# One h @ w_in per later batch on four column groups, spread by transfers, and more groups ahead of the exponentials and the first scores

## The chip, the cores and the metric

The kernel runs on one core of a Trainium2 chip. The metric is the device time of one execution in microseconds (us), as the median of several executions. Five engines run their own queues in order: TensorE (PE in the rows, with its weight loads as PEld), VectorE (DVE), ScalarE (ACT), GpSimd (POOL) and the queue that issues the transfers (SP). They meet at semaphores only.

## The reference, cut to what matters

```python
def mab(q, kv):                                   # attention_out = mab(x, mab(inducing, x))
    s = q @ kv.transpose(0, 2, 1) / np.sqrt(C)
    s = s - s.max(-1, keepdims=True)
    a = np.exp(s)
    a /= a.sum(-1, keepdims=True) + 1e-09
    return a @ kv
h = mab(I, x)                # per batch: 32 inducing points read all 12480 tokens: h is 32 x 128
x = mab(x, h)                # per token: 32 scores, softmax, then a mix of the 32 rows of h
h1 = x @ w_in                # the tokens of 4 batches, 49920 x 128, through 128 x 2048
g = h1 * (1.0 / (1.0 + np.exp(-1.702 * h1)))
out = g @ w_out              # 2048 x 128
```

All is float32, with 4 batches of 12480 tokens. The kernel never forms the attention output: it multiplies `h @ w_in` once per batch (32 x 2048), and the weights of a token's softmax then pick from that product.

## The kernel before, in words

**The main loop.** The tokens lie in blocks of 512, and each block takes eight **groups**, one for every 256 of the 2048 hidden columns; there are 98 blocks, and so 784 groups, numbered `i` from 0 to 783. `first(i)` makes two matmuls `ph<-st,hw` (the softmax weights `st` of the block against `hw`, which is h @ w_in) into one of two `ph` buffers of PSUM, and lets ScalarE write the activation `g`. Its rounded copy `hi` is made by ScalarE from `ph` once more, or by VectorE from `g`; a running account of both engines' costs decides which when the program is built. VectorE then makes the remainder `lo` from `g` and `hi`. `second(i, c)` makes three matmuls into `pso` for each half of a group, six for a group. A `ph` buffer comes free when ScalarE has read it the last time, so the first layer of group i+2 waits for ScalarE's `g` or `hi` of group i.

**The lag.** The second layer of a group follows its first layer by a lag of 6 to 12 half groups. Attention work that takes ScalarE some time hands back the word `LUMP` (line 24): the loop then runs all second-layer work down to a lag of 6 at once, 18 matmuls beyond the usual six, and lets the lag grow again by one half group in every third group. Such a third group has three second-layer matmuls instead of six; I call it a short group. So after each lump 18 groups follow of which six are short.

**Attention in the gaps.** `attention(b)` for batches 1 to 3 is a generator. The loop takes one step of it per group (`next(rest, None)`, line 806), and `hop(n)` inside it stands for n groups of waiting. For one batch it makes, in this order: loads of `xt`; first scores `pa<-xt,indT_sb` of seven pieces of the batch in pairs, copied out by VectorE as `s` with their maximum `mx`; exponentials of four pieces and later three, each with a lump; the weighted sum `pa<-xn,aT`; the small matrix `hT`; second scores `pa<-xt,hT` in pairs, which VectorE transposes into `e` and reduces; their exponentials on ScalarE, of four pieces and then of three, each with a lump. Between gelu and exp ScalarE loads another table each way. `pairs` works through the pieces in the order 0 to 6 for even batches and 6, 0 to 5 for odd ones.

**The lay-out.** `weights_of(b, s)` turns the exponentials of one piece into `st` for four blocks: VectorE sums and divides (`sm`, `e<-e,sm`), transposes to `alT`, ScalarE or VectorE rounds that to `ahT`, VectorE takes the remainder, and 16 transfers spread both. It begins at fixed groups that the loop works out in `begin` (lines 780 to 800): 18, 50, 82, 114, 146, 162, 174, 186, 218 and so on. Where the exponentials that it needs are not yet there, `lay_out` runs the attention generator on until they are (`while key not in es: next(rest)`), and drops what the generator hands back.

**h @ w_in.** `h_w_in(b, c)` makes one of four products of 512 columns. For batches 1 to 3 the table `products` puts them at four groups shortly before and after the batch's first block (186, 188, 190 and 193 for batch 1). `hTs[b]` holds the 32 columns of h four times over, so that each product comes out on all 128 partitions; ScalarE rounds it into `hw`, and VectorE replaces the lower half by the remainder.

Of the kernel before, what the change touches and what calls it, by code (L numbers as in the profile page):

```python
# [8 lines left out]
F32 = mybir.dt.float32  # L9
# [46 lines left out]
def set_attention_then_moe(ctx: ExitStack, tc, xT, x, indT, w_in, w_out, outT):  # L56
# [36 lines left out]
    pe = ctx.enter_context(tc.tile_pool(name="pe", bufs=EB))  # L93
    pt = ctx.enter_context(tc.tile_pool(name="pt", bufs=7))
    pst = ctx.enter_context(tc.tile_pool(name="pst", bufs=G))
    phw = ctx.enter_context(tc.tile_pool(name="phw", bufs=7))
    psm = ctx.enter_context(tc.tile_pool(name="psm", bufs=3))
    ps_h = ctx.enter_context(tc.tile_pool(name="ps_h", bufs=2, space=PSUM))
    ps_o = ctx.enter_context(tc.tile_pool(name="ps_o", bufs=2, space=PSUM))
# [98 lines left out]
    def attention(b):  # L198
# [3 lines left out]
        if not start:  # L202
            for s in range(XB):
                load_xT(b, s)
                yield

        mx = psm.tile([P, NS], F32, tag="mx", name="mx")
        rs = psm.tile([P, NS], F32, tag="rs", name="rs")
# [36 lines left out]
        def maximum(n):  # L245

            mx1 = psm.tile([P, 1], F32, tag="mx1", name="mx1")
            dve.tensor_reduce(mx1, mx[:, 0:n], axis=AX.X, op=ALU.max)
            yield from wait()
            pa = ps_a.tile([P, 512], F32, tag="pa", name="pa")  # L250
            pe_.matmul(pa[0:1, 0:P], mx1, ident, start=True, stop=True)
            yield
            row = psm.tile([1, G, M], F32, tag="row", name="row")
            dve.tensor_reduce(
                row[:, 0, :], pa[0:1, 0:P].rearrange("p (g m) -> p m g", g=G), axis=AX.X, op=ALU.max
            )
            for j in range(1, G):
                dve.tensor_copy(row[:, j, :], row[:, 0, :])
            yield from wait()
            pa = ps_a.tile([P, 512], F32, tag="pa", name="pa")  # L260
            pe_.matmul(pa[:, 0:1], row.rearrange("p g m -> p (g m)"), one, start=True, stop=True)
            yield
            nmx = psm.tile([P, 1], F32, tag="nmx", name="nmx")
            dve.tensor_scalar(nmx, pa[:, 0:1], -scale, None, op0=ALU.mult)
            yield from wait(2)
            return nmx
# [234 lines left out]
            ready.append(True)  # L501
        yield
        for some in (turn[2:],) if start else (turn[0:4], turn[4:]):
            yield from hop(20 if start else 8)
            for pair in pairs(some):
                while full(pair):
                    yield
# [2 lines left out]
                for s, pa in zip(pair, pas):  # L510
                    if s + XB < NS:
                        again(s + XB)
                    mine[s] = yield from second_out(s, pa)
                yield from wait(2)
            for s in some:
                exponentials(s, mine[s])
            yield LUMP

    def h_w_in(b, c):

        if b == 0:
            if c % 2 == 0:
                first_h.append(ps_h.tile([P, 2, 512], F32, tag="ph", name="ph"))
            pa = first_h[-1][:, c % 2]
        else:
            pa = ps_a.tile([P, 512], F32, tag="pa", name="pa")
        pe_.matmul(pa, hTs[b], w_in_sb[:, c * 512:(c + 1) * 512], start=True, stop=True)
        yield
        t = phw.tile([P, 512], F32R, tag="hw", name="hw")
        act.copy(t, pa)  # L530
        dve.tensor_sub(t[P // 2:P], pa[P // 2:P], t[P // 2:P].bitcast(F32))
        hw[b, c] = t

    def weights_of(b, s):

# [217 lines left out]
            yield from attention(b)  # L753

    n = len(work) * NG

    products = []
    for b in range(1, B):
        f = first_block[b, NS - 1 if b % 2 else 0] * NG
        products += [(f + at, b, c) for c, at in enumerate((-6, -4, -2, 1) if b % 2 else (-7, -5, -3, -1))]  # L760
    rest = attentions()
    act.t = dve.t = pe_.t
    back = part = laid = None
    stores = []
    under_way = []
    turns.pop(0)
# [14 lines left out]
    while i < n or under_way:  # L781
        now[0] = i
        if i < n:
# [5 lines left out]
                if turns and first_block[turns[0]] * NG <= i:  # L789
                    back, laid = lay_out()  # L790
            first(i)
            if part is not None:
                run(part)
                part = None
            if products and products[0][0] == i:
                part = h_w_in(*products.pop(0)[1:])
                next(part)
            under_way += [(i, 0), (i, 1)]
            i += 1
        else:  # L800
# [46 lines left out]
```

## Time and profile before

| | |
|---|---|
| median of 3 executions | 1628.84 us (1627.38 to 1629.14) |
| the profiled execution | 1631.19 us, of which its span is 1629.4 us |
| TensorE, VectorE, ScalarE busy | 98%, 83%, 83% of the span |
| chain of work that ended last | TensorE 90%, VectorE 3%, ScalarE 3% |
| first group of the main loop | starts at about 72 us |

A busy share of TensorE in these rows counts matmuls whose modelled ends overlap the next start, so it does not tell whether matmuls follow each other as closely as they can. That is read from the distance between starts, and above all from the distance between the first-layer matmuls `ph<-st,hw` of one group and the next. Counting those from the first one on gives every group its place in time: group 179, for example, starts at 430.73 us.

### The profile page before, as it was taken

The page shows a single profiled execution, that of the slowest core. Times are in us where ns is not written, and L with a number is a line of the kernel's source. Part 1 is how long each engine was busy: PE and PEld are TensorE (multiplying, and loading weights), DVE is VectorE, ACT ScalarE, POOL GpSimd, SP SyncE. Part 2 cuts the span into 40 slices and gives each one's busy share as a digit, 9 for nine tenths or more (in the row PEclk, how much of TensorE's full clock was granted, in tenths as well). Part 3 has the DMA queues.
Part 4 walks back from the last instruction along what each step waited for, and adds up shares of the span by engine and source line. Part 5 has one row for each costly group of instructions (what it writes and reads, how often), then busy time and mean ns, then how long its engine had stood idle before and what let it go on. Part 6 is the DMA issues. An engine that isn't in the chain of part 4 may idle for free.

```text
span 1629.4 us, 21749 instructions
## 1 busy us (share of the span) xinstructions
PE 1593.6 (98%) x7737; PEld 1236.1 (76%) x7737; DVE 1346.0 (83%) x1556; ACT 1352.4 (83%) x1552; POOL 32.0 (2%) x26
## 2 busy tenths in 40 slices
PE   6799999999999999999999999999999999999999
PEld 3577777787777877777777877778778888888887
DVE  6787977888889887788888887878888888888886
ACT  6498888978888888887888888988889988888885
POOL 4300000000000000000000000000000000000000
PEclk9799999999999999999999999999999999999999
DMA  8304218503042114741204101661301011011010
GB/s 338 104 24 159 72 30 187 136 26 98 18 142 84 35 39 86 180 100 39 72 26 190 39 30 46 158 152 40 97 16 48 20 38 46 22 38 45 28 38 20
DMA packets 81946, 126.65 MB, mean 78 GB/s; under 512 B 11632, under 2 KB 50096, under 8 KB 75696
## 3 DMA queue, kind: packets, MB, share of 16 engines
q1 hardware_dynamic: 81840, 125.26, 27.0%
q8 instruction: 63, 1.03, 0.3%
q14 instruction: 43, 0.35, 0.1%
HBM read 74.10 MB, written 25.56 MB: 61 GB/s over the span
## 4 chain that ended last, share of the span: by engine, by line
PE 90%; DVE 3%; ACT 3%; issue 1%; DMA 1%; POOL 1%; SPq 0%; DVEq 0%; ACTq 0%; POOLq 0%
PE pso L46 63%; PE ph L46 22%; PE pa L46 4%; ACT hi L46 1%; DMA xt<-in_xT 1%; ACT g L46 1%; DVE lo L46 1%; DVE e L46 1%; DVE t L46 0%; DVE m L46 0%; ACT s L46 0%; DMA out_T<-ob 0%; DVE alT L46 0%; POOL sq L592 0%; POOL wh L642 0%
## 5 line engine op out<-in xcount | busy, mean ns | idle before, releaser
L46 DVE TENSOR_TENSOR lo<-g,hi 128x1024 fp32r<-128x1024 f32 (+1 forms) x784 | 947.8, 1216 | 156.7 <-ACT hi L46 143.9
L46 ACT ACTIVATE g<-ph 128x1024 f32<-128x1024 f32 (+1 forms) x784 | 805.7, 1033 | 200.3 <-PE ph L46 104.5
L46 PE MATMUL pso<-hi,wl 128*128 128x512 f32 (+1 forms) x1568 | 623.7, 398 | 0.0
L46 PE MATMUL pso<-hi,wh 128*128 128x512 f32 (+1 forms) x1568 | 617.3, 394 | 0.0
L46 PE MATMUL pso<-lo,wh 128*128 128x512 f32 (+1 forms) x1568 | 616.8, 393 | 0.0
L46 PE MATMUL ph<-st,hw 128*128 128x512 f32 x1536 | 491.8, 401 | 8.6 <-ACT hi L46 4.5
L46 ACT ACTIVATE hi<-ph 128x1024 fp32r<-128x1024 f32 (+1 forms) x476 | 488.7, 1027 | 0.0
L46 PEld LDWEIGHTS ph<-st,hw 128*128 128x128 f32 x1536 | 282.0, 188 | 103.1 <-ACT hi L46 16.8
L46 PEld LDWEIGHTS pso<-lo,wh 128*128 128x128 f32 x1568 | 294.4, 188 | 73.3 <-issue 2.9
L46 PEld LDWEIGHTS pso<-hi,wl 128*128 128x128 f32 x1568 | 295.2, 188 | 70.4 <-issue 2.9
L46 PEld LDWEIGHTS pso<-hi,wh 128*128 128x128 f32 x1568 | 294.9, 188 | 70.7
L46 DVE CAST hi<-g 128x1024 fp32r<-128x1024 f32 (+1 forms) x308 | 210.5, 684 | 92.5 <-ACT g L46 92.0
L46 ACT COPY ob<-pso 128x512 f32<-128x512 f32 (+1 forms) x98 | 58.1, 593 | 19.8 <-PE pso L46 19.7
L46 PE MATMUL pa<-xt,indT_sb 128*32 128x512 f32 x192 | 25.8, 641 | 13.5 <-DMA xt<-in_xT 11.1
L46 ACT ACT_TABLE_LOAD x28 | 35.9, 1283 | 2.1 <-PE ph L46 0.9
L46 ACT CAST ahT<-alT 128x512 fp32r<-128x512 f32 (+1 forms) x27 | 15.7, 582 | 14.7 <-DVE alT L46 14.6
L46 PE MATMUL pa<-xt,hT 128*32 128x512 f32 x192 | 25.5, 637 | 1.0 <-DVE hT L46 1.0
L46 PEld LDWEIGHTS pa<-xt,indT_sb 128*32 128x32 f32 x192 | 4.8, 111 | 24.6 <-issue 14.4
L46 ACT ACTIVATE e<-e 128x512 f32<-128x512 f32 (+1 forms) x28 | 14.2, 571 | 9.0 <-DVE e L46 8.9
L46 PEld LDWEIGHTS pa<-xn,aT 128*32 128x32 f32 (+1 forms) x594 | 15.1, 109 | 7.6 <-issue 5.8
L46 PE MATMUL pa<-xn,aT 128*32 128x128 f32 (+1 forms) x594 | 20.7, 276 | 0.0
L46 ACT ACTIVATE s<-s,nmx 128x512 f32<-128x512 f32 (+1 forms) x28 | 18.5, 662 | 2.4 <-DVE nmx L46 2.3
(93 smaller groups left out, 434.3 us busy)
## 6 DMA issues: line engine op xcount, KB each, us to landing
xt<-in_xT SPq DMA_DIRECT2D x48, 1024.0 KB, 7.7
out_T<-ob SPq DMA_DIRECT2D x96, 256.0 KB, 2.0
xn<-in_x SPq DMA_DIRECT2D x72, 256.0 KB, 6.1
st<-ahT SPq DMA_DIRECT2D x192, 64.0 KB, 2.0
st<-alT SPq DMA_DIRECT2D x192, 64.0 KB, 2.0
raw<-in_w_in SPq DMA_DIRECT2D x4, 512.0 KB, 8.9
raw<-in_w_out SPq DMA_DIRECT2D x4, 512.0 KB, 8.1
xt_last<-in_xT SPq DMA_DIRECT2D x4, 96.0 KB, 8.3
```

The costliest lines, as they stand in the source:

```text
L46: return f(*a, **k)
```

## The change

Four things are changed. (1) For batches 1 to 3 the four products of `h_w_in` give way to one `all_h_w_in`: four matmuls with 32 columns of h each, which write to the four quarters of one PSUM tile, so that each 512 columns of the product lie on 32 partitions. One ScalarE copy (`th`) and one VectorE subtraction (`tl`) make the rounded part and the remainder of all four, and 16 transfers on the SP queue write each quarter to all 128 partitions of its `hw` tile. It stands directly after `hT`, some 35 to 40 groups earlier than the products did, and takes the place of `hop(8)` ahead of the second scores. (2) `hop(5)` stands between the loads and the first scores. (3) `hop(3)` stands between the second scores and their exponentials, for batch 0 as well, and the second `hop(8)` becomes `hop(6)`. (4) The `hw` pool gets an eighth buffer and `row` only one.

```diff
@@ -93,7 +93,7 @@
     pe = ctx.enter_context(tc.tile_pool(name="pe", bufs=EB))
     pt = ctx.enter_context(tc.tile_pool(name="pt", bufs=7))
     pst = ctx.enter_context(tc.tile_pool(name="pst", bufs=G))
-    phw = ctx.enter_context(tc.tile_pool(name="phw", bufs=7))
+    phw = ctx.enter_context(tc.tile_pool(name="phw", bufs=8))
     psm = ctx.enter_context(tc.tile_pool(name="psm", bufs=3))
     ps_h = ctx.enter_context(tc.tile_pool(name="ps_h", bufs=2, space=PSUM))
     ps_o = ctx.enter_context(tc.tile_pool(name="ps_o", bufs=2, space=PSUM))
@@ -203,6 +203,7 @@
             for s in range(XB):
                 load_xT(b, s)
                 yield
+            yield from hop(5)
 
         mx = psm.tile([P, NS], F32, tag="mx", name="mx")
         rs = psm.tile([P, NS], F32, tag="rs", name="rs")
@@ -250,7 +251,7 @@
             pa = ps_a.tile([P, 512], F32, tag="pa", name="pa")
             pe_.matmul(pa[0:1, 0:P], mx1, ident, start=True, stop=True)
             yield
-            row = psm.tile([1, G, M], F32, tag="row", name="row")
+            row = psm.tile([1, G, M], F32, tag="row", name="row", bufs=1)
             dve.tensor_reduce(
                 row[:, 0, :], pa[0:1, 0:P].rearrange("p (g m) -> p m g", g=G), axis=AX.X, op=ALU.max
             )
@@ -501,7 +502,7 @@
             ready.append(True)
         yield
         for some in (turn[2:],) if start else (turn[0:4], turn[4:]):
-            yield from hop(20 if start else 8)
+            yield from hop(20) if start else all_h_w_in(b) if 0 in some else hop(6)
             for pair in pairs(some):
                 while full(pair):
                     yield
@@ -512,24 +513,47 @@
                         again(s + XB)
                     mine[s] = yield from second_out(s, pa)
                 yield from wait(2)
+            yield from hop(3)
             for s in some:
                 exponentials(s, mine[s])
             yield LUMP
 
     def h_w_in(b, c):
 
-        if b == 0:
-            if c % 2 == 0:
-                first_h.append(ps_h.tile([P, 2, 512], F32, tag="ph", name="ph"))
-            pa = first_h[-1][:, c % 2]
-        else:
-            pa = ps_a.tile([P, 512], F32, tag="pa", name="pa")
+        if c % 2 == 0:
+            first_h.append(ps_h.tile([P, 2, 512], F32, tag="ph", name="ph"))
+        pa = first_h[-1][:, c % 2]
         pe_.matmul(pa, hTs[b], w_in_sb[:, c * 512:(c + 1) * 512], start=True, stop=True)
         yield
         t = phw.tile([P, 512], F32R, tag="hw", name="hw")
         act.copy(t, pa)
         dve.tensor_sub(t[P // 2:P], pa[P // 2:P], t[P // 2:P].bitcast(F32))
         hw[b, c] = t
+
+    def all_h_w_in(b):
+
+        pa = ps_a.tile([P, 512], F32, tag="pa", name="pa")
+        for c in range(G):
+            pe_.matmul(
+                pa[32 * c:32 * c + 32], hTs[b][:, 0:M], w_in_sb[:, c * 512:(c + 1) * 512],
+                start=True, stop=True,
+            )
+        yield
+        th = pt.tile([P, 512], F32R, tag="t", name="th")
+        act.copy(th, pa)
+        yield
+        tl = pt.tile([P, 512], F32, tag="t", name="tl")
+        dve.tensor_sub(tl, pa, th.bitcast(F32))
+        yield from hop(2)
+        for c in range(G):
+            t = phw.tile([P, 512], F32R, tag="hw", name="hw")
+            for r in range(G):
+                src = th.bitcast(F32) if r < G // 2 else tl
+                nc.sync.dma_start(
+                    t[32 * r:32 * r + 32].bitcast(F32), src[32 * c:32 * c + 32]
+                )
+            hw[b, c] = t
+            yield
 
     def weights_of(b, s):
 
@@ -753,14 +777,9 @@
             yield from attention(b)
 
     n = len(work) * NG
-
-    products = []
-    for b in range(1, B):
-        f = first_block[b, NS - 1 if b % 2 else 0] * NG
-        products += [(f + at, b, c) for c, at in enumerate((-6, -4, -2, 1) if b % 2 else (-7, -5, -3, -1))]
     rest = attentions()
     act.t = dve.t = pe_.t
-    back = part = laid = None
+    back = laid = None
     stores = []
     under_way = []
     turns.pop(0)
@@ -789,12 +808,6 @@
                 if turns and first_block[turns[0]] * NG <= i:
                     back, laid = lay_out()
             first(i)
-            if part is not None:
-                run(part)
-                part = None
-            if products and products[0][0] == i:
-                part = h_w_in(*products.pop(0)[1:])
-                next(part)
             under_way += [(i, 0), (i, 1)]
             i += 1
         else:
```

On TensorE the product moves and changes its shape. The first rows are of the kernel before, at group 186 of batch 1, where `pso` are second-layer and `ph` first-layer matmuls:

```order
L46 MATMUL ph<-st,hw 128x512 x2
L46 MATMUL pa<-w_in_sb,hT 128x512
L46 MATMUL pso<-hi,wl 128x512
L46 MATMUL pso<-lo,wh 128x512
L46 MATMUL pso<-hi,wh 128x512
L46 MATMUL ph<-st,hw 128x512 x2
```

Those of the change, at group 149 of the same batch:

```order
L46 MATMUL pso<-hi,wh 128x512
L46 MATMUL pa<-w_in_sb,hT 32x512 x4
L46 MATMUL ph<-st,hw 128x512 x2
L46 MATMUL pso<-hi,wl 128x512
L46 MATMUL pso<-lo,wh 128x512
```

Twelve wide products, four in each batch, have become three sets of four narrow ones.

On VectorE the first scores of batch 1 move against the lay-out of the piece that begins at group 50. Before, between `lo` of group 49 and that of group 53 (`s` and `mx` belong to the first scores; `sm`, `e<-e,sm` and `alT` to the lay-out):

```order
L46 COPY s_1614<-pa 128x512
L46 TENSOR_REDUCE mx<-s_1614 128x1
L46 TENSOR_TENSOR lo<-g,hi 128x1024
L46 TENSOR_REDUCE sm<-e 128x16
L46 TENSOR_SCALAR sm<-sm 128x16
L46 RECIPROCAL sm<-sm 128x16
L46 TENSOR_TENSOR lo<-g,hi 128x1024
L46 COPY s_1651<-pa 128x512
L46 TENSOR_REDUCE mx<-s_1651 128x1
L46 TENSOR_TENSOR e<-e,sm 128x512
L46 TENSOR_TENSOR lo<-g,hi 128x1024
L46 STREAM_TRANSPOSE alT<-e 128x512
```

With the change, over the same groups:

```order
L46 TENSOR_TENSOR lo<-g,hi 128x1024
L46 COPY s_1612<-pa 128x512
L46 TENSOR_REDUCE mx<-s_1612 128x1
L46 TENSOR_REDUCE sm<-e 128x16
L46 TENSOR_SCALAR sm<-sm 128x16
L46 RECIPROCAL sm<-sm 128x16
L46 TENSOR_TENSOR lo<-g,hi 128x1024
L46 TENSOR_TENSOR e<-e,sm 128x512
L46 TENSOR_TENSOR lo<-g,hi 128x1024
L46 COPY s_1652<-pa 128x512
L46 TENSOR_REDUCE mx<-s_1652 128x1
L46 STREAM_TRANSPOSE alT<-e 128x512
```

The copy of the second score and its maximum now stand in the same group as `alT` and ahead of it; before, they stood a group earlier.

On ScalarE the exponentials of batch 1's first four second scores move from group 163 to group 173. Before (`ob` is the copy of a finished output block):

```order
L46 ACTIVATE g<-ph 128x1024 x2
L46 ACTIVATE hi<-ph 128x1024
L46 ACT_TABLE_LOAD
L46 ACTIVATE e<-e 64x96
L46 ACTIVATE e<-e 128x512 x3
L46 COPY ob<-pso 128x512
L46 ACT_TABLE_LOAD
L46 ACTIVATE g<-ph 128x1024 x2
L46 ACTIVATE hi<-ph 128x1024
L46 CAST ahT<-alT 64x96
```

With the change:

```order
L46 ACTIVATE hi<-ph 128x1024
L46 ACTIVATE g<-ph 128x1024
L46 COPY ob<-pso 128x512
L46 ACT_TABLE_LOAD
L46 ACTIVATE e<-e 64x96
L46 ACTIVATE e<-e 128x512 x3
L46 ACT_TABLE_LOAD
L46 ACTIVATE g<-ph 128x1024 x4
L46 ACTIVATE hi<-ph 128x1024
L46 CAST ahT<-alT 64x96
L46 ACTIVATE g<-ph 128x1024
```

The run of exponentials is the same, but it comes at the point where the lay-out that begins at group 174 asks for them. On TensorE, 24 second-layer matmuls stand in group 163 before, and the six usual ones in groups 173 and 174 with the change: the kernel before has 13 lumps, the changed one 12.

## Rows read from the trace of the kernel before

**Rows 1.** The first section of the page of the profile: busy time, share of the span and instructions of each engine.
```profile
PE 1593.6 (98%) x7737; PEld 1236.1 (76%) x7737; DVE 1346.0 (83%) x1556; ACT 1352.4 (83%) x1552; POOL 32.0 (2%) x26
```

**Rows 2.** The chain of work that ended last in order of time, in a stretch without attention work. The columns are start, duration (both us) and what ran; `pso` x6 is the second layer of a group.
```profile
503.18 1.40 PE pso L46 x6
505.05 1.40 PE pso L46 x6
```

**Rows 3.** The same view at the second of batch 2's four products of h @ w_in, one product being two matmul records.
```profile
852.10 0.86 PE pa L46 x2
```

**Rows 4.** The timeline of TensorE around a lone set of four 32-column matmuls with 512 columns each (eight records), batch 3's last second score, in group 569, which is a short group. The columns are start, duration (us), engine, line, operation and operands.
```profile
1214.36 0.62 PE L46 MATMUL ph<-st,hw 128*128 128x512 f32 x2
1215.60 1.06 PE L46 MATMUL pa<-xt,hT 128*32 128x512 f32 x8
1216.60 0.74 PE L46 MATMUL ph<-st,hw 128*128 128x512 f32 x2
```

**Rows 5.** The timeline around batch 1's last second score (group 179, a short one): rows of TensorE, among them the first and the last of nine matmul starts that follow the late first layer (a `ph` row there holds two), then four of ScalarE. In brackets stands the idle time of the engine just before, and what ended it.
```profile
430.73 0.62 PE L46 MATMUL ph<-st,hw 128*128 128x512 f32 x2
431.98 1.07 PE L46 MATMUL pa<-xt,hT 128*32 128x512 f32 x8
435.04 0.73 PE L46 MATMUL ph<-st,hw 128*128 128x512 f32 x2 [2.00 <-ACT hi L46]
...
436.07 0.60 PE L46 MATMUL pso<-hi,wh 128*128 128x512 f32 x1
...
439.46 0.42 PE L46 MATMUL pso<-hi,wh 128*128 128x512 f32 x1
...
428.41 1.03 ACT L46 ACTIVATE g<-ph 128x1024 f32<-128x1024 f32 x1
429.31 1.04 ACT L46 ACTIVATE hi<-ph 128x1024 fp32r<-128x1024 f32 x1
432.89 0.27 ACT L46 CAST ahT<-alT 64x96 fp32r<-64x96 f32 x1 [2.54 <-DVE alT L46]
433.98 1.00 ACT L46 ACTIVATE hi<-ph 128x1024 fp32r<-128x1024 f32 x1
```

**Rows 6.** Sums over stretches of time: from:to, length, busy time and instructions of each engine, then the granted share of TensorE's clock (the first number after POOL), the share of DMA and GB/s. The first stretch follows the stall of Rows 5, the second lies in the start of the kernel.
```profile
436.10:439.50 3.40, 3.40 (x10) 2.63 (x9) 2.94 (x5) 2.27 (x3) 0.00 (x0) 0.50 0.00 0
53.80:64.00 10.20, 6.56 (x23) 2.42 (x24) 7.04 (x16) 1.35 (x3) 3.18 (x3) 0.50 0.25 89
```

**Rows 7.** TensorE's timeline at other places where a first layer came late, one after the other: the starts of groups 86 to 88 (86 is a short one); of group 397, behind the first pair of first scores of batch 3, which stands in group 396, with the start of 396 and the second half of the pair; and of groups 572 and 573 (572 is a short one).
```profile
244.98 0.63 PE L46 MATMUL ph<-st,hw 128*128 128x512 f32 x2
246.54 0.73 PE L46 MATMUL ph<-st,hw 128*128 128x512 f32 x2 [0.23 <-ACT hi L46]
249.47 0.73 PE L46 MATMUL ph<-st,hw 128*128 128x512 f32 x2 [0.81 <-ACT g L46]
...
868.64 0.63 PE L46 MATMUL ph<-st,hw 128*128 128x512 f32 x2
872.13 1.07 PE L46 MATMUL pa<-xt,indT_sb 128*32 128x512 f32 x8 [0.46 <-DMA xt<-in_xT]
873.13 0.73 PE L46 MATMUL ph<-st,hw 128*128 128x512 f32 x2
...
1220.67 0.74 PE L46 MATMUL ph<-st,hw 128*128 128x512 f32 x2
1222.48 0.74 PE L46 MATMUL ph<-st,hw 128*128 128x512 f32 x2 [0.39 <-ACT hi L46]
```

**Rows 8.** The timeline from group 49 to 56 (55 is a short one), where the third pair of batch 1's first scores meets the lay-out that began at group 50: rows of VectorE, then ScalarE's `ahT` and TensorE's pair and next first layer.
```profile
174.20 0.68 DVE L46 COPY s<-pa 128x512 f32<-128x512 f32 x1
...
175.53 1.22 DVE L46 TENSOR_TENSOR lo<-g,hi 128x1024 fp32r<-128x1024 f32 x1
176.66 0.68 DVE L46 TENSOR_REDUCE sm<-e 128x16 f32<-128x512 f32 x1
...
177.75 1.16 DVE L46 TENSOR_TENSOR lo<-g,hi 128x1024 fp32r<-128x1024 f32 x1
...
180.14 0.68 DVE L46 TENSOR_TENSOR e<-e,sm 128x512 f32<-128x512 f32 x1
180.74 1.22 DVE L46 TENSOR_TENSOR lo<-g,hi 128x1024 fp32r<-128x1024 f32 x1
181.88 0.70 DVE L46 STREAM_TRANSPOSE alT<-e 128x512 f32<-128x512 f32 x1
...
182.62 0.62 ACT L46 CAST ahT<-alT 128x512 fp32r<-128x512 f32 x1 [2.18 <-DVE alT L46]
...
181.59 1.92 PE L46 MATMUL pa<-xt,indT_sb 128*32 128x512 f32 x16
184.21 0.73 PE L46 MATMUL ph<-st,hw 128*128 128x512 f32 x2 [0.70 <-ACT g L46]
```

**Rows 9.** ScalarE's timeline at the lump of group 184: table load, three exponentials, table load.
```profile
445.87 1.28 ACT L46 ACT_TABLE_LOAD   x1
447.17 1.68 ACT L46 ACTIVATE e<-e 128x512 f32<-128x512 f32 x3
448.86 1.28 ACT L46 ACT_TABLE_LOAD   x1
```

**Rows 10.** The timeline of the SP queue: one of the 16 transfers of a lay-out.
```profile
379.47 0.59 SPq L572 DMA_DIRECT2D st<-ahT  x1
```

## The prediction, made blind

> **What bounds the kernel now.** I read the page first: TensorE is busy for 98% of the span and the two engines behind it for 83% each [rows 1]. That share does not tell whether TensorE ever waits, so I went to the chain of waits. Where no attention work runs, one second layer starts 1.87 us after the one before [rows 2]. The six matmuls of a second layer take 1.40 us there, 0.233 us each, and two more for the first layer make up the 1.87 us. A short group then takes 1.17 us. In such stretches no group deviates from this, with ScalarE and VectorE less busy, so TensorE is the bound. What a change can gain is matmul time that it takes away, and idle time of TensorE between groups. I found the idle time by holding every group's start against 1.87 us plus the attention matmuls in it. The places are in [rows 5], [rows 7] and [rows 8], and in most of them one thing is seen: ScalarE's queue stands at `ahT`, which waits for VectorE's `alT`, and the next first layer waits for a `ph` buffer that ScalarE has not read yet.
>
> **The product itself.** One wide product costs the chain 0.86 us [rows 3], and the twelve 10.3 us. Four matmuls of 32 columns, shape for shape those of a second score, stand alone in group 569: from its first layer to the next 2.24 us pass, 1.07 us more than a short group has [rows 4]. Three such sets cost 3.2 us, so 7.1 us go. The Trainium skill, in "TensorEngine Tiling (Array Packing)", section "Theoretical Speedup", gives up to four times for 32 columns. By that a set would cost 0.86 us and 7.7 us would go. Its section "Key Properties" speaks against the change: switching the tiling drains the array. By the rows the first layer behind a set takes 0.74 us where 0.62 us is usual [rows 4], and that is inside the 1.07 us. I stay with the row.
>
> What surrounds the product lies beside TensorE. ScalarE makes one copy of 128x512 as long as `ahT`, 0.62 us [rows 8], in place of four, and VectorE one subtraction in place of four. The 16 transfers cost the SP queue 0.59 us each [rows 10], 9.4 us per batch. In batch 1 they alternate with the 16 of the lay-out of group 146, of which all but the last four go out at once, so the queue is busy for some 17 us from group 153 on, to about group 162. The lay-out's first tile is due at group 160 and has the second place in that queue, and `hw` is not read before group 192. This costs nothing; a stall of a first layer on `st` would be the sign that it does. The buffers `hw` and `row` are written long after their last readers, which I also take at nothing.
>
> **Idle time that goes.** (a) The late first layer of batch 1: 435.04 minus 430.73 us is 4.31 us, where a short group and a set of four would be 2.24 us; 2.05 us were lost [rows 5]. ScalarE had waited 2.54 us for `alT`, because VectorE was still at the second scores. Behind that the clock is granted at 0.50, the lower of its two levels (1.2 of 2.4 GHz), for 3.4 us [rows 6]; eight matmuls take 3.39 us instead of 1.87 us [rows 5], so 1.5 us more are lost. The change moves this second score from group 179 to 187: 3.55 us go. (b) Groups 86 to 88 lose 0.4 and 1.05 us in the same way, a lay-out among short groups [rows 7]; with the lump at group 87 instead of 79 the lay-out of group 82 meets full groups, and 1.45 us go. (c) Batch 3's first scores wait for the loads, 4.49 us against 1.87 plus the pair's 1.92 us [rows 7, 8]; with `hop(5)` the loads have over 9 us more, and 0.7 us go. (d) Group 573 comes 0.64 us late [rows 7]; the lump moves by three groups, and by the working below 0.2 us of it is left. Together with the product, 13.2 us go.
>
> **Idle time that comes.** The steps of the attention move by 3 to 11 groups, the lay-outs not at all, so they meet at other places. I worked each place out by hand, as a list of starts, with these steps: `g` and `hi` 0.90 us from start to start on ScalarE [rows 5], `lo` 1.14, `s` with `mx` 1.33, `sm` with its two followers 1.09, `e<-e,sm` 0.60, `alT` 0.7 us on VectorE [rows 8]. Tried on group 56 of the kernel before, the same working gives 0.6 us where 0.70 us of idle time is seen [rows 8].
>
> First place, group 56 in batch 1, counted from the start of group 49. That is now a short group and holds the first pair, so group 50 starts at 3.1 us, and 56 would start at 12.9 us. VectorE gets `g` of group 50 at 4.9. With `hi`, `lo`, `s` and `mx`, `sm`, `lo`, `e<-e,sm`, `lo` it is at 12.1 us. Now `s` and `mx` of the pair's second score come ahead of `alT`, which ends at 14.1. `ahT` ends at 14.6, `g` and `hi` of group 54 at 16.6, and group 56 has waited for them 3.75 us. A shorter stall than this was followed by the slow clock in (a), so I add 1.5 us; the 0.75 us that the place costs already come off: 4.5 us.
>
> Second place, group 174. The lay-out asks for batch 1's exponentials just when the generator would hand back the lump, and drops it. ScalarE then has `ob`, a table load, four exponentials and a table load between `g` of 173 and `g` of 174: 1.3, 1.9 and 1.3 us [rows 9] behind an `ob` of 0.55 us that follows the last `pso`. Before, 18 extra matmuls of 4.2 us covered this. Without them `g` of 174 ends 6.3 us after the start of group 174, and group 176, due after 3.75 us, loses 2.5 us, and 1.5 us for the clock: 4.0 us.
>
> Third place, groups 192 and 193. The last second score, now in group 187, meets the lay-out of group 186, and VectorE comes from a pair of scores with no gap. `alT` ends 9.4 us after the start of 187, `hi` of 190 at 11.9; group 192 was due at 10.4 and loses 1.45 us, group 193 another 0.3 us. I add no slow clock: 1.7 us. Small ones by the same working: 0.45 us at group 120, and 0.35 us each at 224 and 416, where the second pair of first scores now stands two groups ahead of a lay-out: 1.15 us. Sum of what comes: 11.35 us.
>
> The balance is 13.2 minus 11.35, or 1.9 us less. The profiled execution took 1631.2 us with a span of 1629.4 us, the median is 1628.84 us; I take the difference over to the median: **1626.9 us**. A difference of 0.2%, 3.3 us, is about what a measurement here can tell from none.
>
> **Rivals.** *The places are milder than worked out.* If the clock stays at its upper level and the two collisions cost what collisions cost before (0.75 us each), then 0, 2.5, 0.75 and 1.15 us come, 4.4 us in all. The time is 1628.84 minus 8.8, 1620.0 us. For it speaks that stalls of 1.05 us and less were not followed by the slow clock; against it, that the working names VectorE's steps one by one and hit the known place.
>
> *Slower: the slow clock lasts.* At 53.8 us it was granted at 0.50 for 10.2 us in one piece [rows 6]. If the stalls at groups 56 and 174 are followed by that instead of 3.4 us, each costs 3.0 us more in proportion, and the balance turns to plus 4.1 us: 1632.9 us. It decides from some 9 us per place on, where each costs 4.1 us. Against it: the only instance in the main loop lasted 3.4 us, and TensorE has work at once after a stall.
>
> *The change doesn't do what it says:* if the four narrow matmuls don't run beside each other, a set costs as much as four wide ones, 7.1 us are not saved, and 1634.0 us come out. [Rows 4] speak against it.
>
> **How the numbers follow.** I give the balance 55%: it lies between 1623.8 us (no slow clock, 3 us less) and 1629.5 us, mostly within 0.2%. The milder places get 25%, the lasting clock 9%, the serial product 3%, and 8% are left for places that I did not find, to both sides. That makes 0.37 for faster, 0.49 for no difference, 0.14 for slower. The range reaches to the milder case below, and to 1631.5 us above, beyond which most of the two slower cases lie.
>
> **What would show it.** In the profile after, the sets of `pa<-w_in_sb,hT` should cost some 1.07 us from group to group; the `ahT` of the lay-out of group 50 should wait for `alT` and group 56 start late by 3 to 4 us; the exponentials of batch 1 should stand without a run of 24 second-layer matmuls, with group 176 late; and the granted clock should fall behind both. Batch 3's first scores should find their loads landed. If groups 56 and 176 start on time, or the clock does not fall, I am wrong in the direction of 1620 us.

## The result, and the profile after

| | before | after |
|---|---|---|
| median | 1628.26 us (1627.38 to 1629.14, 4 runs) | 1643.2 us (1641.9 to 1646.5, 4 runs) |
| the profiled execution | 1631.19 us, span 1629.4 us | 1642.66 us, span 1640.9 us |

The ratio is 1.0095, with a 95% interval of 1.0077 to 1.0112: the change makes the kernel slower by about 15 us. The prediction was 1626.9 us with a range up to 1631.5 us.

The busy times hardly move; this is the first section of the page after, to be held against [rows 1]:

```profile
PE 1591.9 (97%) x7737; PEld 1233.6 (75%) x7737; DVE 1336.4 (81%) x1544; ACT 1352.3 (82%) x1546; POOL 32.8 (2%) x26
```

TensorE has the same number of matmuls and 1.7 us less busy time in a span that is 11.5 us longer, so most of the time went into waits. The starts of groups 32, 224 and 420 and the ends of both traces tell where (the predicted column sorts the terms of the prediction by batch):

| stretch | predicted | after less before |
|---|---|---|
| start to group 32 (132.31, now 130.61 us) | 0 | -1.7 |
| groups 32 to 224, batch 1 (523.09, now 534.97 us) | +3.6 | +13.6 |
| groups 224 to 420, batch 2 (917.14, now 928.51 us) | -2.7 | -0.5 |
| group 420 to the end, batch 3 | -2.8 | +0.1 |
| sum | -1.9 | +11.5 |

**Batch 1's weighted sum was not in the prediction at all.** The timeline of TensorE in group 96:

```profile
267.48 0.40 PE L46 MATMUL pso<-hi,wh 128*128 128x512 f32 x1
272.61 1.94 PE L46 MATMUL pa<-xn,aT 128*32 128x128 f32 x32 [4.73 <-DMA xn<-in_x]
274.47 1.22 PE L46 MATMUL ph<-st,hw 128*128 128x512 f32 x2
```

TensorE waits 4.73 us for the first piece of x, and the sum itself then runs at half the pace (1.94 us; a sum of the same 32 matmuls takes 1.08 us at the upper level of the clock). The SP queue tells why the piece is late; the last line is of the kernel before:

```profile
259.64 0.51 SPq L596 DMA_DIRECT2D st<-ahT  x1
...
262.74 0.59 SPq L596 DMA_DIRECT2D st<-alT  x1
263.37 0.59 SPq L596 DMA_DIRECT2D st<-ahT  x1
264.00 0.59 SPq L596 DMA_DIRECT2D st<-alT  x1
264.64 2.20 SPq L175 DMA_DIRECT2D xn<-in_x  x4
266.94 0.51 SPq L596 DMA_DIRECT2D st<-ahT  x1
...
241.38 6.36 SPq L175 DMA_DIRECT2D xn<-in_x  x8
```

The four loads `xn` are issued at 264.64 us, behind the first twelve transfers of the lay-out that began at group 82; the matmul that needs them is due at 267.7 us. Eight of the twelve go out directly ahead of the loads, from 259.64 us on, and hold the queue for 5.0 us, about as long as TensorE waits. Before, the loads of the first two pieces were issued together at 241.38 us, ahead of all sixteen.

**The three places that the prediction named are there.** The timelines of TensorE, VectorE and ScalarE around group 56:

```profile
178.44 0.40 PE L46 MATMUL pso<-hi,wh 128*128 128x512 f32 x1
182.14 0.80 PE L46 MATMUL ph<-st,hw 128*128 128x512 f32 x1 [3.31 <-ACT hi L46]
...
177.58 0.68 DVE L46 COPY s<-pa 128x512 f32<-128x512 f32 x1
178.29 0.69 DVE L46 TENSOR_REDUCE mx<-s 128x1 f32<-128x512 f32 x1
178.90 0.70 DVE L46 STREAM_TRANSPOSE alT<-e 128x512 f32<-128x512 f32 x1
...
179.63 0.62 ACT L46 CAST ahT<-alT 128x512 fp32r<-128x512 f32 x1 [2.28 <-DVE alT L46]
180.16 1.02 ACT L46 ACTIVATE g<-ph 128x1024 f32<-128x1024 f32 x1
181.07 1.01 ACT L46 ACTIVATE hi<-ph 128x1024 fp32r<-128x1024 f32 x1
```

It reads as worked out: `s` and `mx` ahead of `alT`, ScalarE standing at `ahT`, then `g` and `hi`, then the first layer. From one matmul start to the next there are 3.70 us where 0.23 us is usual: 3.47 us lost, 3.75 us predicted, and 0.75 us in [rows 8]. At group 176, without the lump, ScalarE's queue and the first layer behind it:

```profile
429.10 1.28 ACT L46 ACT_TABLE_LOAD   x1
430.40 1.85 ACT L46 ACTIVATE e<-e 64x96 f32<-64x96 f32 x4
432.26 1.28 ACT L46 ACT_TABLE_LOAD   x1
433.56 1.94 ACT L46 ACTIVATE g<-ph 128x1024 f32<-128x1024 f32 x2
...
434.63 0.80 PE L46 MATMUL ph<-st,hw 128*128 128x512 f32 x1 [2.47 <-ACT g L46]
```

By starts that is a stall of 2.62 us, predicted 2.5 us. Group 192, the third place, starts 1.57 us late, predicted 1.45 us; another 0.31 us lie between the first two matmuls of its first layer, and group 193, predicted 0.3 us late, has no wait of its own. ScalarE's `ahT` and TensorE's first layer there:

```profile
468.20 0.62 ACT L46 CAST ahT<-alT 128x512 fp32r<-128x512 f32 x1 [1.57 <-DVE alT L46]
...
470.71 0.97 PE L46 MATMUL ph<-left,hw 128*128 128x192 f32 x4 [1.40 <-DMA st<-ahT]
```

**Two more places were not seen**, in batch 2 (group 384) and in batch 3 (group 584):

```profile
854.00 0.70 DVE L46 STREAM_TRANSPOSE alT<-e 128x512 f32<-128x512 f32 x1
...
854.73 0.62 ACT L46 CAST ahT<-alT 128x512 fp32r<-128x512 f32 x1 [1.05 <-DVE alT L46]
...
856.32 0.74 PE L46 MATMUL ph<-st,hw 128*128 128x512 f32 x2 [1.43 <-ACT g L46]
...
1252.85 0.69 DVE L46 CAST hi<-g 128x1024 fp32r<-128x1024 f32 x1 [4.11 <-ACT g L46]
...
1257.18 0.70 DVE L46 STREAM_TRANSPOSE alT<-e 128x512 f32<-128x512 f32 x1
...
1257.92 0.62 ACT L46 CAST ahT<-alT 128x512 fp32r<-128x512 f32 x1 [1.92 <-DVE alT L46]
1258.45 1.02 ACT L46 ACTIVATE g<-ph 128x1024 f32<-128x1024 f32 x1
1259.36 1.01 ACT L46 ACTIVATE hi<-ph 128x1024 fp32r<-128x1024 f32 x1
...
1260.43 0.98 PE L46 MATMUL ph<-left,hw 128*128 128x192 f32 x4 [2.02 <-DMA st<-ahT]
```

By starts they cost 1.59 and 2.17 us. In the second one VectorE had lost 4.11 us at a lump whose table loads now fall on the beginning of the lay-out of group 578, so `alT` came late. The rows of groups 192 and 584 name a transfer as what TensorE waited for. It was not: these matmuls read `left` and not `st`, the named transfers land at 470.80 and 1260.79 us, after the matmuls have begun, and at group 584 `hi` ends at 1260.37 us, just ahead of the matmul.

The granted clock (the first number after POOL) behind these places, as sums over stretches:

```profile
181.60:185.00 3.40, 2.86 (x7) 2.29 (x8) 2.88 (x3) 3.23 (x4) 0.00 (x0) 0.50 0.04 10
270.40:277.20 6.80, 4.59 (x39) 3.69 (x40) 0.09 (x1) 1.47 (x2) 0.00 (x0) 0.50 1.23 213
434.20:437.60 3.40, 2.97 (x7) 2.40 (x8) 2.89 (x6) 2.32 (x3) 0.00 (x0) 0.50 0.00 0
471.80:475.20 3.40, 3.40 (x12) 2.82 (x11) 2.90 (x4) 2.34 (x4) 0.00 (x0) 0.50 0.22 53
854.50:858.00 3.50, 2.07 (x9) 1.41 (x8) 2.96 (x4) 3.27 (x5) 0.00 (x0) 1.00 0.28 94
1258.00:1262.00 4.00, 1.92 (x10) 1.24 (x9) 2.58 (x3) 3.85 (x5) 0.00 (x0) 1.00 0.09 20
```

Leaving out the first groups of the main loop, up to 81.1 us, where both kernels have the lower level as well, these are four stretches at that level, against the one of [rows 6]; the last two stalls are followed by none. The product, finally, costs what [rows 4] let expect. The timeline of TensorE in batch 1:

```profile
378.90 0.39 PE L46 MATMUL pso<-hi,wh 128*128 128x512 f32 x1
379.21 1.06 PE L46 MATMUL pa<-w_in_sb,hT 128*32 128x512 f32 x8
380.21 0.73 PE L46 MATMUL ph<-st,hw 128*128 128x512 f32 x2
```

That is 1.31 us between the starts of the neighbours in place of 0.23 us, 1.08 us for a set, and the two other sets cost 1.08 us too. The sets stand in groups 149, 339 and 531, which is 37, 46 and 47 groups ahead of the batch's first wide product before.

### The profile page after: what moved, and what is told of

Read it like the earlier page. It is cut to its first block, busy times and chain, and to the rows that moved or that the text cites. A ratio compares the mean times of both kernels' runs of the same rounds, so it can differ in the third digit from the quotient of the medians.

```text
span 1640.9 us, 21800 instructions
## 1 busy us (share of the span) xinstructions
PE 1591.9 (97%) x7737; PEld 1233.6 (75%) x7737; DVE 1336.4 (81%) x1544; ACT 1352.3 (82%) x1546; POOL 32.8 (2%) x26
## 3 DMA queue, kind: packets, MB, share of 16 engines
q8 instruction: 63, 1.03, 0.3%
## 4 chain that ended last, share of the span: by engine, by line
PE 67%; DVE 2%; ACT 2%; issue 1%; DMA 0%; DVEq 0%; ACTq 0%
PE pso L46 48%; PE ph L46 17%; PE pa L46 2%; DVE lo L46 1%; ACT hi L46 1%; ACT g L46 1%; DVE e L46 0%; DVE alT L46 0%; DVE hi L46 0%; DMA out_T<-ob 0%; DMA st<-ahT 0%; DVE sm L46 0%; DVE s L46 0%; ACT ob L46 0%; ACT ahT L46 0%
## 5 line engine op out<-in xcount | busy, mean ns | idle before, releaser
L46 ACT CAST ahT<-alT 128x512 fp32r<-128x512 f32 (+1 forms) x27 | 15.4, 571 | 20.6 <-DVE alT L46 20.6
```

Of the source, the lines that this page charges most:

```text
L46: return f(*a, **k)
```

## The experiments

**Theory A**: the product gains what was predicted, and the loss comes from where the extra waiting puts the attention steps: against the lay-outs on VectorE and ScalarE, and behind their transfers on the SP queue. **Rivals**: the new way of making the product costs it (B), x is late for another reason (C), the stall at 432 us has another cause than the dropped lump (D).

### One half of the change each

The product alone has neither wait, and `hop(8)` as before (the edit is against the change):

```diff
-            yield from hop(5)
...
-            yield from hop(20) if start else all_h_w_in(b) if 0 in some else hop(6)
+            yield from hop(20) if start else all_h_w_in(b) if 0 in some else hop(8)
...
-            yield from hop(3)
```

> The kernel before with the one narrow product and its 16 transfers per batch, directly after hT in place of hop(8); no hop(5), no hop(3), the second hop(8) as before. Theory A (the loss comes from where the steps of the attention now stand against the lay-outs and in the SP queue, and the product itself gains 7.1 us): about 1621 us, 1618 to 1624. Rival B (the product's new way, with its early copies and its 16 transfers on the SP queue, is what costs): 1635 us or more. In the profile, A expects a set of four narrow matmuls to cost 1.1 us and batch 1's weighted sum to find its x loaded.

Measured: 1625.37 us, ratio 0.9972 (0.9962 to 0.9983). The waits alone, put into the kernel before:

```diff
+            yield from hop(5)
...
-            yield from hop(20 if start else 8)
+            yield from hop(20 if start else 8 if 0 in some else 6)
...
+            yield from hop(3)
```

> The kernel before with hop(5) ahead of the first scores, hop(3) ahead of the exponentials and hop(6) for the second hop(8); the four wide products per batch stay where they were. Theory A: all of the loss and none of the gain, about 1650 us, 1645 to 1654. Rival B: near the kernel before, 1626 to 1632 us.

Measured: 1646.39 us, ratio 1.0102 (1.0087 to 1.0117). Its trace has four stalls of the change: 3.47 us at 178 us, 4.9 us of waiting for `xn`, 2.62 us at 431 us and 1.56 us at 857 us. Two places differ: near the third place, at 465 us, a wide product waits 2.16 us until VectorE has made `hw` of the one before, and batch 3's stall at group 584 is missing. B falls. The product alone is 4.6 us faster than the kernel before by its ratio, at a time 1.4 us above what A expected.

### The late loads

First the loads were issued from GpSimd's queue, where no lay-out stands ahead of them:

```diff
-            nc.sync.dma_start(
+            nc.gpsimd.dma_start(
                 t[32 * j:32 * j + 32, 0:w // 32],
```

> The changed kernel, with the loads of x for the weighted sum (load_x) issued by GpSimd's queue, which is idle then, and not by SP. Theory A says that these loads stood behind the 16 transfers of the lay-out of group 82 in the SP queue, and that this costs some 5.7 us of waiting and about 1.3 us of slow clock in batch 1: about 1636 us, 1634 to 1638, and the first weighted sum of batch 1 no longer waits. Rival C (the loads are late because the data path is full or x is asked for too late): no change, 1643 us, and the wait for x stays.

Measured: 1643.33 us, ratio 1.0081 (1.0066 to 1.0096), outside what A expected. The weighted sum was on time again and its slow clock gone, but the first group of the main loop started at 79.86 in place of 70.92 us, which takes back more than the late loads had cost. The timelines of TensorE and of GpSimd in this kernel:

```profile
79.86 2.05 PE L46 MATMUL ph<-st,hw 128*128 128x512 f32 x4 [8.92 <-DMA st<-alT]
...
60.69 5.37 POOL L175 DMA_DIRECT2D xn<-in_x  x8 [0.31 <-POOL wl L637]
```

and the sums over the stretch between:

```profile
71.00:79.00 8.00, 0.00 (x0) 0.00 (x0) 1.05 (x2) 2.07 (x3) 0.00 (x0) 0.66 1.03 207
```

Nothing holds GpSimd back, so it asks for batch 1's x at 60.69 us, 180 us sooner than the kernel before does. The DMA engines are then full (share 1.03), and the first lay-out's transfers wait among them: the first one lands 8.4 us after its issue, in the change 2.0 us. The Trainium skill, in "DMA: Bandwidth & Descriptors", section "Issuing engines are not separate DMA queues", says that transfers started by the scalar, sync or gpsimd engine end up on the same 16 DMA engines and interleave; these rows agree. So the loads were then asked for on SP, but sooner, ahead of the maximum, which tests A without that:

```diff
+            xns = [load_x(b, 0), load_x(b, 1)]
             nmx = yield from maximum(NS)
...
-            xn = load_x(b, 0)
+            xn = xns.pop(0)
...
-                    later = load_x(b, s + 1)
+                    later = xns.pop(0) if xns else load_x(b, s + 1)
```

> The changed kernel, with the loads of the first two pieces of x for the weighted sum asked for before the maximum is worked out, some ten groups sooner, and so on the SP queue ahead of the 16 transfers of the lay-out of group 82. Theory A (batch 1's first weighted sum waited for its data because its loads stood behind those transfers, and the slow clock of 6.8 us came after that stall): the wait of 4.7 us and the slow clock at 270 us are gone, the start of the kernel stays as it is, and about 8 us go: 1633 to 1638 us. Rival D (the lost time is only moved: what the sum no longer waits for, the next lay-out waits for): the sum is on time, and the total stays at 1640 to 1645 us.

Measured: 1635.92 us, ratio 1.0039 (1.0026 to 1.0053). The loads go out at 215.15 us, 25 groups sooner than in the change (some ten were expected), and the sum takes 1.08 us again:

```profile
215.15 6.40 SPq L175 DMA_DIRECT2D xn<-in_x  x8
...
268.31 1.08 PE L46 MATMUL pa<-xn,aT 128*32 128x128 f32 x32
```

and no slow clock follows. Group by group, the trace of this kernel differs from that of the change almost only at groups 96 and 97, by 5.67 and 1.04 us. These 6.7 us are the price of the late loads, slow clock included, and the rival that the loss only moves on falls. This run alone doesn't tell C from A, since the loads are now both sooner and ahead of the transfers. Their landings do: from the first issue to the last landing a piece's four loads take 7.8 us in the change (264.64 to 272.47 us), 7.8 us here and 7.9 us in the kernel before. So the data path was no slower, and without the 5.0 us of transfers ahead of them the loads would have landed at about 267.5 us, in time. C falls.

### The dropped lump

Here the loop runs a lump that the lay-out took from the generator:

```diff
-            next(rest)
+            if next(rest) is LUMP:
+                asked.append(key)
...
-        if i < n and next(rest, None) is LUMP:
+        if i < n and (next(rest, None) is LUMP or asked):
+            asked.clear()
```

> The changed kernel, with lay_out telling the loop when the generator hands back a lump, so that the 18 extra second-layer matmuls are run in group 174. Theory A: the 2.6 us of idle time and 1.3 us of slow clock near 432 us go, unless the short groups that follow bring a new collision: about 1639 us, 1637 to 1643. Rival D (the late first layer there has another cause, the exponentials being covered anyway): no change, 1643 us, with the same idle time at the same place.

Measured: 1639.36 us, ratio 1.0065 (1.0047 to 1.0082). The stall at 432 us and its slow clock are gone, so D falls; but a stall of 2.46 us stands at 530.7 us where the change has 0.62 us, where ScalarE stands at `ahT` of the lay-out of group 218 for 2.43 us.

### Which of the waits it is

The change without `hop(5)`, and the change without `hop(3)`:

> The changed kernel without the five groups ahead of the first scores; the three ahead of the exponentials and the product stay. Theory A (the loss of batch 1 comes from hop(5), by way of the pair of scores that meets the lay-out of group 50 and of the loads that go behind that of group 82): group 56 is on time, the weighted sum costs 1.1 us, and with 4.8 and about 8 us gone the time is 1629 to 1634 us. Rival E (the three groups ahead of the exponentials are enough for the loss, since they move all that follows): 1637 to 1644 us.

> The changed kernel without the three groups ahead of the exponentials; hop(5) and the product stay. The first loads of x then go to the SP queue ahead of the lay-out of group 82 again, and batch 1's exponentials of the first four pieces come before the lay-out of group 174 asks for them, but the first scores meet the lay-out of group 50 as in the change. Theory A: the weighted sum is on time (8 us less), no stall at group 176 (4 us less), the stall of 3.5 us at group 56 stays: 1628 to 1634 us. Rival E (the places are a matter of chance, and others take their place): 1636 to 1643 us.

Measured, with the product alone and the change beside them, all as ratios to the kernel before (the product alone also has `hop(8)` where the other three have `hop(6)`):

| | without `hop(3)` | with `hop(3)` |
|---|---|---|
| without `hop(5)` | 0.9972 (0.9962 to 0.9983) | 1.0019 (1.0010 to 1.0028) |
| with `hop(5)` | 0.9976 (0.9967 to 0.9985) | 1.0095 (1.0077 to 1.0112) |

In us the medians of the two are 1631.86 without `hop(5)` and 1625.08 without `hop(3)`. So `hop(5)` by itself costs nothing that can be told, `hop(3)` by itself some 8 us (1.0019 less 0.9972), and both together 20 us: 11 to 12 us come only when both shift the same steps. With either alone the weighted sum is on time, and group 56 loses 1.26 us (no `hop(5)`) or 0.74 us (no `hop(3)`) in place of 3.47 us. What `hop(3)` alone costs is seen in the trace without `hop(5)` mainly in batches 2 and 3: first scores wait 2.72 and 1.24 us for the loads of `xt`, and stalls of 1.55 and 2.17 us stand at 842 and 1246 us. E falls for both. Without `hop(5)` the time is as A expected, without `hop(3)` 2.9 us below what A expected, for A had expected the stall at group 56 to stay. It did not, since batch 0 has no `hop(3)` there either and all that follows comes three groups sooner: the pairs stand in groups 46 and 53 and not in 49 and 56 (3.10 us from the start of 46 to that of 47; in the change 3.11 us from 49 to 50), and so meet the lay-out of group 50 in another step.

### The wait at the head of ScalarE's queue

Apart from the late loads and the dropped lump, the stalls of the change had one form, ScalarE standing at `ahT`. If that is the cause and not a want of time on both engines (F), a later `ahT` takes them away wherever the attention steps stand:

```diff
         give_back(slot)
-        yield
+        yield from hop(1 if (b, s) == (0, 0) else 3)
```

With the product alone:

> The product by four column groups alone, and in every lay-out ScalarE's or VectorE's copy ahT (with the transfers behind it) two groups later than now, so that ScalarE's queue doesn't come to it before alT is made. Theory A (the stalls that are left, some 6 us in all, are ScalarE standing at ahT until VectorE has made alT): most of them go, 1620 to 1623.5 us, 1.5 to 5 us below the product alone. Rival F (the first layer waits because both engines have more work than time there, whoever's turn it is): the stalls move by two groups and stay as long, 1624 to 1627 us. Rival G (the transfers come too late for their blocks): first layers wait for st, over 1628 us.

Measured: 1623.37 us, ratio 0.9967 (0.9955 to 0.9979); that it is faster than the product alone can't be told from this. All stalls of over 0.45 us outside the attention's own matmuls are gone, which speaks against F, and no first layer waits for `st`, so G falls. What was won is given back, though, at batch 2's first scores. The loads of `xt` stand behind the lay-out's transfers in both kernels, but these now come two groups later: the loads go out at the start of group 203 (471.25 us), with the product alone at the end of group 199 (471.81 us). TensorE's timeline there, and the sums behind it:

```profile
476.32 1.06 PE L46 MATMUL pa<-xt,indT_sb 128*32 128x512 f32 x8 [2.17 <-DMA xt<-in_xT]
...
480.03 1.94 PE L46 MATMUL pa<-xt,indT_sb 128*32 128x512 f32 x8 [2.65 <-DMA xt<-in_xT]
```

```profile
477.00:484.00 7.00, 4.35 (x18) 2.11 (x15) 0.32 (x3) 0.84 (x1) 0.00 (x0) 0.55 0.86 362
```

The same edit in the kernel before:

> The kernel before, and in every lay-out ahT with the transfers behind it two groups later; nothing of the change. Theory A: the stalls at 245, 433 and 1222 us with their slow clock go (5 to 6 us), but the first scores of batches 2 and 3 then wait for xt, whose loads go behind the lay-out's later transfers, some 6 and 3 us as in the product with ahT later: 1627 to 1632 us, and so the product by four column groups is worth 5 to 8 us here too. Rival B (the later ahT is what helps, and the product is worth nothing): 1620 to 1625 us.

Measured: 1627.98 us, ratio 0.9992 (0.9983 to 1.0001), with the same wait for `xt`. The product is worth 0.9992 less 0.9967, some 4 us, between these two, a little less than A expected; that it is worth nothing falls.

The change itself, with its waits, the later `ahT` and the sooner loads:

> The changed kernel with both: the loads of x sooner and ahT two groups later. All groups of waiting stay where the change put them. Theory A (the places cost what they cost because ScalarE stands at ahT): the stalls of 3.5 us at group 56, 1.6 us at group 192, 1.6 us in batch 2 and 2.2 us in batch 3 go with the slow clocks behind them, and the dropped lump's 2.6 us stay: 1622 to 1630 us. Rival F (the engines have more work than time there): 1632 to 1638 us, as with the loads alone.

Measured: 1618.7 us, ratio 0.9936 (0.9923 to 0.9950), below even what A expected. The groups of ScalarE's `ahT` in the change and in this kernel (busy, mean ns of one, idle time before):

```profile
L46 ACT CAST ahT<-alT 128x512 fp32r<-128x512 f32 (+1 forms) x27 | 15.4, 571 | 20.6 <-DVE alT L46 20.6
```

```profile
L46 ACT CAST ahT<-alT 128x512 fp32r<-128x512 f32 (+1 forms) x26 | 15.1, 581 | 0.0
```

20.6 us of standing are gone, and with them all stalls of over 0.6 us outside the attention's own matmuls but one: the dropped lump's 2.62 us, to the hundredth as in the change. F falls. Here `hop(5)` does what it is for: the loads of `xt` land in time although the lay-out's transfers come later.

### All three mends

> The changed kernel with three mends: the loads of x sooner, ahT two groups later, and a lump that the lay-out took from the generator is run after all by the loop. Theory A: the last stall that the two mends left, 2.6 us at group 176, and the slow clock behind it go, about 4 us: 1614 to 1617 us. Rival D (24 second-layer matmuls more in a row bring short groups to places where they weren't, and a new stall takes the place of the old, as a stall of 2.5 us did when the lump alone was kept): 1617 to 1621 us.

Measured: 1614.65 us, ratio 0.9914 (0.9901 to 0.9928). No stall of over 0.6 us outside the attention's own matmuls is left, and no slow clock after 80 us. The time is as A expected, and the rival that a kept lump brings a new stall falls. Without `hop(3)`:

> The changed kernel with all three mends and without the three groups ahead of the exponentials. Theory A (those groups only moved attention steps onto the lay-outs; with ahT two groups later nothing is left there to lose or gain): as with them, 1613 to 1617 us. Rival H (the three groups give the exponentials time and are worth something in themselves): 1618 to 1623 us.

Measured: 1612.3 us (1612.04 to 1614.99), ratio 0.9905 (0.9891 to 0.9918), the fastest of all and 0.7 us below what A expected, though the two intervals overlap. H falls: the groups ahead of the exponentials are worth nothing in themselves.

## Why the prediction was wrong, point by point

- *The product*, 7.1 us to go: right in kind and nearly in size. A set costs 1.08 us between its neighbours and 0.11 us in the group behind it, a wide product 0.86 us, so three batches save 12 x 0.86 less 3 x 1.19, 6.8 us. By the ratios two pairs of kernels show 4 to 5 us of it, and the waits alone against the change 1.1 us, where the change has the stall at group 584 besides. The row's 1.07 us came about, but I took the slower first layer behind a set to lie inside it, and it comes on top, with 0.11 us. The four times that the Trainium skill gives as the most, in "TensorEngine Tiling (Array Packing)", section "Theoretical Speedup", did not come about: 3.44 us for four wide products against 1.19 us for a set is 2.9 times.
- *What surrounds the product* at nothing: right; no first layer waits for `hw` or, the two misnamed rows aside, for `st`, and the buffers cost nothing.
- *Idle time that goes*: (a) to (d) went, but (a) only because the waits moved the second score; with the product alone the same stall stays.
- *The three named places*: stalls of 3.47, 2.62 and 1.88 us where 3.75, 2.5 and 1.75 us were worked out. For the third I added no slow clock, and one of 3.4 us came, with five matmuls at 0.43 us in place of 0.23 us and a slower first layer behind them: some 1.6 us too little.
- **The step that failed is "idle time that comes": its list of places was taken for complete.** I followed the moved steps through VectorE and ScalarE for three places and a few small ones, but of the SP queue only the new transfers of `hw`. That the loads of x, moved by eight groups, fall behind a lay-out's transfers was not looked at, and so put at nothing; it cost 6.7 us, the largest single term. In batches 2 and 3 only what goes was worked out with care; the collisions at groups 384 (1.6 us) and 584 (2.2 us) were not. Together with the clock at the third place that is 12.1 of 15.1 us. The 15.1 us are the 13.4 us between the balance and the trace and the 1.7 us by which the start, where no moved step lies, was shorter.
- *The slower rival* named a lasting slow clock. One of 6.8 us did come, but behind the late loads and not at groups 56 and 176, where it lasted 3.4 us each time. Against this rival I had set that the only instance in the main loop lasted 3.4 us. That was misread: the first groups of the loop, from 74.3 to 81.1 us, had the lower level for 6.8 us in one piece in the kernel before. The 8% for places not found was put to both sides; all that was found lay on one.

Some 3 us of the difference, 1.7 of them in batch 1, remain in small steps that I did not assign. The profiled execution of before was 3 us above its median, so a sum against it is also no better than that.

## What to carry to other kernels

Where a change shifts a chain of steps against others that keep their place, list for every shifted instruction what it passes on every queue, transfers included, for all repetitions: the costs here came from crossings, and two shifts that cost nothing and 8 us apart cost 20 us together. An instruction that waits for another engine at the head of an in-order queue is better put later in the program than hurried: two groups of delay for `ahT` took 20.6 us of standing away, and with the other two mends `hop(3)` cost nothing that can be told. What stands behind such an instruction on another queue has to have the time for it: without `hop(5)` the loads of `xt` came late and gave the gain back. A load can be asked for too soon as well as too late: 180 us sooner, in the start of the kernel, cost 8.9 us; 49.5 us sooner than in the change cost nothing.

## What the runs showed of the hardware that was not expected

Up to about 2.5 us, how long a stall was did not decide whether the clock fell behind it. Batch 1's last second score stalls in the product alone as in [rows 5], 1.99 us, and the stretch behind it has the upper level; in the kernel before it has the lower one [rows 6]. The rows of the product alone, TensorE's timeline and the sums:

```profile
434.25 0.73 PE L46 MATMUL ph<-st,hw 128*128 128x512 f32 x2 [1.99 <-ACT hi L46]
```

```profile
434.20:437.60 3.40, 3.35 (x14) 2.70 (x15) 2.94 (x4) 3.40 (x4) 0.00 (x0) 1.00 0.00 0
```

The stall of 2.17 us at group 584 is the same in the change, with the upper level behind it, and in the change without `hop(5)`, with the lower one:

```profile
1249.70:1253.10 3.40, 3.40 (x11) 2.84 (x11) 3.37 (x5) 1.69 (x3) 0.00 (x0) 0.52 0.19 45
```

The Trainium skill, in "TensorE: Matmul & The Clock Gate", section "What's actually happening", says that how many matmuls run at the lower clock varies from run to run of the same kernel. These rows compare two kernels each and don't show that by themselves; the eight runs of the product alone agree with it, for their mean granted clock lies between 0.991 and 0.997, and the trace above is of the one with 0.997. What decides it is left open by these runs. A term for the slow clock behind a stall of about 1.5 to 2.5 us is thus a chance and not a sum: it came behind 1.57 us at group 192, and not behind 2.46 us with the lump kept. Behind all stalls of 2.6 us and more in these traces it came; the three stretches of 3.4 us in the change cost 1.4 to 1.6 us each. How long it lasts is not given by the stall either: the 3.47 us at group 56 were followed by 3.4 us of it in the change and by 6.8 us in the kernel with the loads on GpSimd.
